# A fused retention and SoLU kernel: four more activation tiles transposed by DMA, the extra load buffers one stage sooner, and the orders of all engines renewed from the fifth step on

## The chip, the cores and the metric

The kernel runs on one core of a Trainium2 chip. A core has five engines that run side by side and meet at semaphores: TensorE (PE, matrix products; PEld is its row of weight loads), VectorE (DVE), ScalarE (ACT), GpSimd (POOL) and SyncE (SP, which here issues nearly all transfers to the 16 DMA engines). The metric is device time in microseconds (us), less is better.

## The reference

Two parts follow each other. The first is attention with a decay (retention) for 8 batches and 8 heads, a sequence of 576 and a head size of 64. The second takes the 4608 tokens by 512 features that come out, multiplies by `w_in` (512 x 1024), applies SoLU (h times its softmax), normalizes, scales with `g_ln` and multiplies by `w_out` (1024 x 512).

```python
scores = scale * np.matmul(q, k.transpose(0, 1, 3, 2))
Dmat = np.where(rel >= 0, gamma[:, None, None] ** rel[None, :, :], 0.0)
ret = np.matmul(scores * Dmat[None, :, :, :], v)
...
h = x @ w_in
e = np.exp(h - h_max)
sm = e / (np.sum(e, axis=-1, keepdims=True) + 1e-09)
solu = h * sm
ln = (solu - mu) / np.sqrt(var + 1e-06) * g_ln
out = ln @ w_out
```

All inputs and the output are float32; the matrix products run in float16 with sums in float32.

## The kernel before

**Stages and tiles.** The retention is cut into 18 windows. Sixteen hold 256 positions of one batch, two (the last of each half of the batches) gather the 64 positions that remain of four batches. Each window is done in two halves of four heads: 36 stages. Each window then gives two tiles of 128 tokens for the second part: 36 tiles. The two run interleaved, a stage runs some three steps ahead of the tile with the same number.

A stage i consists of these operations (in brackets the lines in the code that the profile shows):
- `ldq`, `ldk`, `ldv` (L462, L467): loads of q, k and v by SP, into five `raw` buffers of each kind, or, for the stages that `extra(i)` names, into three more (`bis`). These three take the space of the buffers through which the weights came in, so they cannot be used before `w2_center` (`wc`, L853) has read the last of these.
- `sq`, `sk`, `cv` (L477, L482): scaling of q and k with the decay and the cast of v to float16, most of it on POOL, a few of the first ones on DVE and ACT.
- `T` (L509 in the first ten stages, L519 later): PE transposes q and k; `Te` or `TL` (L547, L549) on ACT copies the result from PE's memory to an `ev` buffer, of which there are eight.
- `S` (L619): the scores, into the bank `s`; `mask` (L655) on DVE multiplies with the mask.
- `K` (L579): the update of the state from k and v; `st`, `sm`, `sc` (L679 to L682, L687, L696) carry it on, on DVE and POOL.
- `I` and `V` (L579): the part from the state and the part from the scores, summed in the bank `xy`; `xe` (L701) on ACT casts the result to `xT`.

A tile t consists of these:
- `M1` (L712): eight matmuls with `w_in` into the bank `h`; `ex` (L720), the exponential, on ACT; `so` (L735, L730), the product, on DVE, which frees `h`. There is a single `h`, so M1 of a tile waits for `so` of the tile before.
- the statistics: `bnA`, `bnB` (L741, L743) on DVE or `va` (L749) on ACT, then `fx`, `fin` and `rs` (L758, L764, L775).
- the transpose of solu, in one of two ways. Either PE does it (`L`, L531 for the first four and the last tile, L538 with 32 narrow matmuls for the others) and ACT copies it out; or, for the tiles in the list `LX`, one DMA transpose does it (`lx`, L567), issued by SP, from the buffer of solu straight to an `ev` buffer. Where PE does it in the steady part, tile t shares one transposed block and one copy (`TL`, 128x1024) with stage t + 6; where it doesn't, stage t + 6 is copied alone (`Te`, 128x512).
- `M2` (L785): eight matmuls with `w_out`, most of the time into the same bank `s` that the scores use, so that `S` waits for the copy before it; `oe` (L794) on ACT scales and copies the result, `out` (L805, L810) stores it.

**What sets the order.** The order of every engine is written out by hand in `ORDER` (L53 to L110), a string of names for each engine. `plan()` gives each operation its dependencies and its buffers; `order_ops` merges the five lists into one order of emission with a table of durations. Engines run their lists strictly in order, and SP's list is also the order in which transfers are issued. So an operation that waits holds up everything behind it in its own list. `LX` (L42) and `R0` (L44) are read by `ev_T`, `ev_L` and `extra`:

```python
def ev_T(i):
    return f"tx{i}" if i in TX else f"Te{i}" if i < NJ + 2 or i - 6 in LX else f"TL{i - 2}"
...
def extra(i):
    return i >= R0 and (i - R0) % 8 >= 5
```

With `R0 = 10`, stages 15 to 17, 23 to 25 and 31 to 33 are loaded into the extra buffers. With `LX` from 14, tiles 14 to 34 are transposed by DMA; tiles 4 to 13 are transposed on PE together with stages 10 to 19. In the list of PE, a step from M1 to M1 looks like this in the part where PE transposes solu, and like this later:

```
M1_11 M2_7 I14 L10 V14 T16 S15 M1_12
...
M1_24 M2_20 I27 T29 V27 K29 S28 M1_25
```

Of the kernel before, what the change touches and what calls it, by code (L numbers as in the profile page):

```python
# [12 lines left out]
I32 = mybir.dt.int32  # L13
# [4 lines left out]
for _b in range(0, B, 4):  # L18
# [20 lines left out]
)  # L39


LX = (14, 15, 16, 17, 18, 19, 20, 21, 22, 23, 24, 25, 26, 27, 28, 29, 30, 31, 32, 33, 34)  # L42
TX = ()
R0 = 10  # L44
OT = 30
SPL = ()
TWO = ()
# [4 lines left out]

ORDER = dict(  # L53
    PE=(
# [11 lines left out]
    ),  # L66
    ACT=(
# [9 lines left out]
    ),  # L77
    DVE=(
# [9 lines left out]
    ),  # L88
    POOL=(
# [8 lines left out]
    ),  # L98
    SP=(
# [9 lines left out]
    ),  # L109
)  # L110

# [8 lines left out]
def ev_T(i):  # L120
    return f"tx{i}" if i in TX else f"Te{i}" if i < NJ + 2 or i - 6 in LX else f"TL{i - 2}"


def ev_L(t):
    return f"lx{t}" if t in LX else f"Le{t}" if t < NJ - 4 or t + 6 >= NS or t + 6 in TX else f"TL{t + 4}"


def extra(i):
    return i >= R0 and (i - R0) % 8 >= 5

# [18 lines left out]
def plan():  # L149
# [3 lines left out]
    def op(name, eng, kind, deps, key, bufs=(), moved=0.0):  # L153
        eng = ON.get(name, eng)
        dur = DUR[kind[eng] if isinstance(kind, dict) else kind] if not isinstance(kind, float) else kind
        ops.append(Op(name, eng, dur, deps, rank.get(name, OFF + PER * key[0] + key[1]), bufs, moved))

    for i in range(NS):
# [21 lines left out]
        else:  # L180
            sdep = [f"sc{2 * (w - 8 + 2 * r + 1) + hf}" for r in range(4)]
        jn, alone = i >= NJ + 2, i - 6 in LX
        if i in TX:
# [15 lines left out]
    for t in range(NT):  # L199
# [4 lines left out]
        op(f"ex{t}", "ACT", "ex", [f"M1_{t}"], (m, 3.3), [("e", [f"so{t}"])])  # L204
        op(f"so{t}", "DVE", "soA" if va else "so", [f"ex{t}"], (m, 4.56), [("solu", [f"lx{t}" if t in LX else f"L{t}", f"va{t}" if va else f"bnB{t}"])])
        if va:
# [10 lines left out]
        early = t < NJ - 4  # L217
        if t in LX:
            op(f"lx{t}", "SP", "lx", [f"so{t}"], (m + 2, 0.1), [("ev", [f"M2_{t}"])], DUR["ltx"])
        lasts = [x for x in range(NT) if NJ - 4 <= x < OT and ev_L(x)[:2] == "Le"]  # L220
        after = [f"Te{NJ + 1}", f"Le{NJ - 5}"] if t == NJ - 4 else []
        if t in lasts:
            after += [f"Le{t - 2}" if t - 2 in lasts else ev_T(max(i for i in range(NS) if i not in TX))]
        if t not in LX:
            op(f"L{t}", "PE", "Lw" if wide(f"L{t}") else "L", [f"so{t}"] + after, (m + 2, 0.1),
# [855 lines left out]
```

## Time and profile before

| | |
|---|---|
| median of 3 runs | 210.38 us (209.81 to 211.48) |
| the profiled execution | 210.31 us |
| its span, first to last instruction | 208.6 us |
| PE, DVE, ACT, POOL busy | 95%, 73%, 68%, 67% of the span |
| PE's clock granted | 0.999 of full speed |
| HBM read, written | 32.56 MB, 9.44 MB |

The profile is of one execution. An engine's busy time counts its own instructions, not the waits, the branches or the issue of transfers. In the timeline a row is one instruction or several of a kind in a row: start, length, engine, line, operation, what is written from what, with shapes and the count; in brackets stands the idle time before it and what ended that. A row of windows gives for one stretch of time the busy time of each engine and the number of its instructions. The share of DMA is the time of the packets that start in the stretch over 16 engines, and so can pass 1 where packets queue.

### The profile page before, as it was taken

The numbers are of one execution on the slowest core, as the hardware profiler recorded it, in microseconds if no ns is written. First come the engines' busy times: TensorE is split into PE (matmuls) and PEld (weight loads), VectorE is DVE, ScalarE is ACT, GpSimd is POOL, SyncE is SP. The second block draws the span as 40 slices with busy tenths as digits, with TensorE's granted clock in tenths as the row PEclk, the third lists the DMA queues.
The fourth block names the chain that finished last, engine by engine and source line by source line (L and its number), as shares of the span: only waits on it lengthen the run. The fifth ranks groups of instructions, "written<-read, shape, count | busy, mean of one in ns | idle before, by whom it ended". The sixth has DMA issues, their size and how long they took to land. (4 is left out here: it accounts for less than half of the span.)

```text
span 208.6 us, 8795 instructions
## 1 busy us (share of the span) xinstructions
PE 197.4 (95%) x3704; PEld 109.3 (52%) x3704; DVE 151.7 (73%) x269; ACT 142.6 (68%) x250; POOL 139.9 (67%) x235
## 2 busy tenths in 40 slices
PE   7998898899999999999999999999999999999981
PEld 2353553665555556566555555555565555544441
DVE  6476868996868788688876877687688787728550
ACT  2367677898667667766787678667768966468441
POOL 7444648999995999677559997996996593201110
PEclk9999999999999999999999999999999999999999
DMA  6999999999756766999999999989997869917834
GB/s 164 340 361 300 326 314 264 301 294 304 226 169 199 205 191 207 287 293 284 201 304 286 221 290 237 225 217 288 220 155 213 198 162 187 175 53 172 142 141 104
DMA packets 86889, 48.09 MB, mean 231 GB/s; under 512 B 25400, under 2 KB 80704, under 8 KB 86848
## 3 DMA queue, kind: packets, MB, share of 16 engines
q1 hardware_dynamic: 86608, 47.33, 90.9%
q8 instruction: 29, 0.48, 1.0%
q10 hardware_dynamic: 240, 0.18, 0.4%
q14 instruction: 12, 0.10, 0.2%
HBM read 32.56 MB, written 9.44 MB: 201 GB/s over the span
## 5 line engine op out<-in xcount | busy, mean ns | idle before, releaser
L712 PE MATMUL h_ps<-w_in,xT 128*128 128x512 f16 x288 | 68.6, 380 | 0.2 <-ACT xT L701 0.2
L785 PE MATMUL o_ps<-w2c,ev 128*128 128x512 f16 (+1 forms) x296 | 67.6, 373 | 0.0
L655 DVE TENSOR_TENSOR ret<-s_ps,masks 128x1024 f16<-128x1024 f32 x36 | 43.8, 1218 | 13.1 <-PE s_ps L619 13.0
L720 ACT ACTIVATE e_sb<-h_ps 128x1024 f32<-128x1024 f32 x36 | 36.8, 1023 | 17.6 <-PE h_ps L712 17.0
L785 PEld LDWEIGHTS <-ev 128*128 128x128 f16 x296 | 28.8, 98 | 32.9
L477 POOL TENSOR_TENSOR k<-rawk,small 128x512 f16<-128x512 f32 x34 | 35.3, 1046 | 8.9 <-DMA rawk<-in_k_dram 8.4
L712 PEld LDWEIGHTS <-xT 128*128 128x128 f16 x288 | 25.4, 98 | 29.6 <-ACT xT L701 1.0
L735 DVE TENSOR_TENSOR solu<-h_ps,e_sb 128x1024 f16<-128x1024 f32 x22 | 26.9, 1222 | 17.7 <-ACT e_sb L720 17.7
L794 ACT ACTIVATE o_sb<-o_ps,rs 128x512 f32<-128x512 f32 (+1 forms) x37 | 24.8, 675 | 21.8 <-PE o_ps L785 10.2
L477 POOL TENSOR_TENSOR q<-rawq,small 128x512 f16<-128x512 f32 x34 | 35.3, 1043 | 5.6 <-DMA rawq<-in_q_dram 5.0
L701 ACT CAST xT<-xy 128x512 f16<-128x512 f32 x36 | 26.4, 735 | 4.9 <-PE xy L579 4.7
L741 DVE BATCH_NORM_STATS2 bs<-solu 128x6 f32<-128x512 f16 x44 | 29.5, 682 | 0.1
L696 POOL CAST sbd<-gg 64x256 f16<-64x256 f32 x64 | 25.3, 395 | 2.6
L549 ACT COPY ev<-tl 128x512 f32<-128x512 f32 (+1 forms) x26 | 19.5, 749 | 2.7 <-PE tl L519 2.5
L730 DVE SCALAR_TENSOR_TENSOR solu<-h_ps,e_sb 128x1024 f16<-128x1024 f32 x14 | 17.1, 1223 | 5.0 <-ACT e_sb L720 3.8
L775 POOL TENSOR_TENSOR rs<-w,small 128x2 f32<-128x2 f32 x18 | 12.4, 690 | 11.6 <-DVE w L764 10.6
L482 POOL CAST v<-rawv 128x512 f16<-128x512 f32 x28 | 17.0, 610 | 3.8 <-DMA rawv<-in_v_dram 3.5
L687 POOL TENSOR_TENSOR gg<-gt,small 128x128 f32<-128x128 f32 x32 | 13.1, 409 | 6.6 <-DVE gt L682 6.5
L773 POOL TENSOR_TENSOR w<-mv,w 128x2 f32<-128x2 f32 x11 | 2.1, 195 | 22.8 <-DVE mv L743 8.0
L749 ACT ACTIVATE junk<-solu,su 128x1024 bf16<-128x1024 f16 x14 | 16.1, 1149 | 0.1
L619 PE MATMUL s_ps<-ev 64*64 64x128 f16 x576 | 15.1, 220 | 0.5 <-ACT o_sb L794 0.2
L579 PE MATMUL xy<-ret,v 64*64 64x128 f16 x576 | 15.0, 220 | 0.1
(73 smaller groups left out, 216.1 us busy)
## 6 DMA issues: line engine op xcount, KB each, us to landing
rawq<-in_q_dram SPq DMA_DIRECT2D x32, 256.0 KB, 5.3
rawk<-in_k_dram SPq DMA_DIRECT2D x32, 256.0 KB, 5.5
rawv<-in_v_dram SPq DMA_DIRECT2D x32, 256.0 KB, 5.4
out_dram<-o_sb SPq DMA_DIRECT2D x32, 256.0 KB, 3.7
wst<-in_moe_w_in_dram SPq DMA_DIRECT2D x4, 512.0 KB, 6.7
wst<-in_moe_w_out_dram SPq DMA_DIRECT2D x4, 512.0 KB, 8.6
rawq<-in_q_dram SPq DMA_DIRECT2D x16, 64.0 KB, 3.4
rawk<-in_k_dram SPq DMA_DIRECT2D x16, 64.0 KB, 3.2
```

Of the source, the lines that this page charges most:

```text
L477: eng.tensor_tensor(out=t.rearrange("p j h d -> p h j d"), in0=st[i]["r" + nm], in1=g, op=ALU.mult)
L549: nc.scalar.copy(out=t[:, lo:hi].rearrange("p x (r w) -> p r x w", r=2), in_=tls[n].rearrange("p r x w -> p (r x w)").bitcast(FP).rearrang ...
L655: nc.vector.tensor_tensor(out=d["ret"].rearrange("p e h j q -> p (e h) (j q)")[:, :, 0:n], in0=d["s"].rearrange("p e h j q -> p (e h) (j q ...
L696: nc.gpsimd.tensor_copy(out=t[ee[e], :, :, ee[e]], in_=st[i]["gg"][ee[e]])
L701: nc.scalar.copy(out=xT[:, 2 * w : 2 * w + 2, 2 * hf : 2 * hf + 2].rearrange("p c h (q j) -> p c h j q", j=2), in_=xys[i][:, :, 0:256].rea ...
L712: nc.tensor.matmul(out=h_ps[:, hh], lhsT=xT[:, t, dc], rhs=w_in16[:, dc, hh], start=(dc == 0), stop=(dc == 3),)
L720: nc.scalar.activation(out=d["e"], in_=d["h"], func=ACT.Exp, accum_out=se[:, t : t + 1])
L730: nc.vector.scalar_tensor_tensor(out=d["solu"], in0=d["h"], scalar=1.0, in1=d["e"], op0=ALU.mult, op1=ALU.mult, accum_out=d["su"],)
L735: nc.vector.tensor_tensor(out=d["solu"], in0=d["h"], in1=d["e"], op=ALU.mult)
L741: nc.vector.bn_stats(out=d["bs"][:, half], in_=d["solu"][:, half * 512 : half * 512 + 512])
L785: nc.tensor.matmul(out=o, lhsT=d["ev"][:, d["lo"] + c], rhs=w2c16[:, c, mm], start=(c == 0), stop=(c == 7))
L794: nc.scalar.activation(out=d["osb"][:, mm], in_=d["o", half], func=ACT.Copy, scale=ws[t // 2]["rs"][:, t % 2 : t % 2 + 1])
```

## The change

1. `LX` begins with 10 instead of 14: tiles 10 to 13 are transposed by DMA too. Their `L` leaves PE (128 narrow matmuls), `TL14` to `TL17` on ACT become `Te16` to `Te19`, and `lx10` to `lx13` come into the list of SP.
2. `R0` is 9 instead of 10: the extra load buffers serve stages 14 to 16, 22 to 24 and 30 to 32.
3. `ORDER` is written anew. The lists agree up to `M1_3` on PE, `Te5` on ACT, `so1` on DVE, `sq4` on POOL and `ldq6` on SP, and differ in many places after that.

The core of the diff, with the part of the lists where they begin to differ and where the four transposes stand (in the lists of the diff, lines that go on are cut):

```diff
-LX = (14, 15, 16, 17, 18, 19, 20, 21, 22, 23, 24, 25, 26, 27, 28, 29, 30, 31, 32, 33, 34)
+LX = (10, 11, 12, 13, 14, 15, 16, 17, 18, 19, 20, 21, 22, 23, 24, 25, 26, 27, 28, 29, 30, 31, 32, 33, 34)
 TX = ()
-R0 = 10
+R0 = 9
...
PE
-M1_3 T5 K7 T6 I4 S5 V4 T7 I5 S6 V5 T8 M1_4 I6 S7 V6 K8 T9 L2 M2_0 I7 L3 V7 K9 S8 M1_5 M2_1 I8 L4 V8 K10 S9 T10
+M1_3 K7 T5 I4 V4 S5 T6 I5 V5 S6 T7 M1_4 T8 I6 S7 V6 K8 L2 T9 M2_0 L3 I7 V7 S8 K9 M1_5 M2_1 I8 V8 L4 T10 K10 S9
...
-M1_11 M2_7 I14 L10 V14 T16 S15 M1_12 M2_8 I15 L11 V15 T17 S16 M1_13 M2_9 I16 V16 L12 T18 K18 S17
+M1_11 M2_7 I14 T16 V14 S15 M1_12 M2_8 I15 V15 T17 S16 M1_13 M2_9 I16 V16 K18 T18 S17
-M1_14 M2_10 I17 L13 V17 T19 S18 K19 M1_15
+M1_14 M2_10 I17 T19 V17 K19 S18 M1_15
ACT
-Te5 va2 Te6 xe4 fx1 fx0 Te7 xe5 va0 Te8 ex4 xe6 Le2 va3 oe0 xe7 Le3 Te9 ex5 oe1 TL8 xe8 ex6
+Te5 va0 xe4 Te6 fx1 xe5 fx0 Te7 va3 va2 Te8 xe6 Le2 ex4 oe0 Te9 xe7 ex5 Le3 oe1 xe8 TL8 fx2 ex6
POOL
-sk4 sq4 sk6 sm4 sc4 sk5 sm6 sk7 sm5 sq5 sc5 sq6 sq7 sk8 sq8 sk9 sc6 cv8 sq9 sm7 sc7 rs0 sq10
+sk4 sq4 sm4 sk6 sk5 sc4 sm6 sk7 sq5 sm5 sc6 sq6 sc5 sq7 sq8 cv8 sk8 sq9 sk9 sm7 cv9 rs0 sc7
...
-sc9 sq12 sm10 sq13 sk14 sk13 sc10 sk12 cv12 sm11 rs2 cv13 sc11 sq15
+sc9 sq12 sm10 sk12 cv12 sc10 sk14 sm11 rs2 sk13 sq14 cv15 sc11 sq13
SP
-out4 ldv17 out6 out5 ldv19 ldq19 ldk19 ldk20 ldv20 ldq20 ldv21 ldq22 ldk21 out8 out7 ldq21 ldv22 ldk22
+out4 ldq17 ldv20 ldv19 ldq19 ldq20 ldk19 ldk20 out5 out6 lx10 ldq21 ldv21 ldk21 ldk23 ldv23 ldq23 lx11 out7
+ldv22 ldk22 lx12 out8 out9 ldq22 ldq24 ldk25 out10 ldk24 lx13 ldv24 ldq25 ldk26 lx14
```

Nothing else is changed: the operations, their shapes, the numbers of buffers and the code that emits them are the same.

88 rows, old and new, of tables (ACT, DVE, PE, POOL) are left out of this document.

## The prediction

> **What bounds the kernel now.** I read the page's first two parts, then the stages by windows, then one step of the timeline.
>
> ```profile
> span 208.6 us, 8795 instructions
> ...
> PE 197.4 (95%) x3704; PEld 109.3 (52%) x3704; DVE 151.7 (73%) x269; ACT 142.6 (68%) x250; POOL 139.9 (67%) x235
> ...
> DMA  6999999999756766999999999989997869917834
> ```
>
> PE is busy for 95% of the span, and its gaps lie in the start and the tail. The DMA digits show full load up to slice 10, slack in slices 10 to 15 (52 to 83 us), and full load again after that. A step of the pipeline runs from one M1 (the eight w_in matmuls, L712) to the next, and step t begins with M1_t. The windows below are steps 11 to 14, the last four in which PE transposes a solu tile (L10 to L13); after them come the sums of steps 15 to 18 and of 28 to 30, where the queue of SP does it by DMA. Columns: length, busy time and count of each engine, PE clock, DMA share, GB/s.
>
> ```profile
> 79.30:84.19 4.89, 4.89 (x127) 2.80 (x116) 3.60 (x6) 3.77 (x8) 4.77 (x8) 1.00 0.80 249
> 84.19:89.42 5.23, 5.09 (x123) 2.87 (x117) 3.86 (x5) 3.42 (x6) 3.46 (x6) 1.00 1.03 280
> 89.42:94.49 5.07, 5.07 (x142) 3.04 (x137) 4.58 (x7) 3.11 (x6) 3.24 (x5) 1.00 0.99 291
> 94.49:99.51 5.02, 5.02 (x142) 3.04 (x137) 3.64 (x8) 3.62 (x7) 4.27 (x8) 1.00 0.98 292
> sum 20.21, PE 20.07 PEld 11.75 DVE 15.68 ACT 13.92 POOL 15.74; mean PE 5.02 PEld 2.94 DVE 3.92 ACT 3.48 POOL 3.93
> ...
> sum 19.23, PE 19.23 PEld 10.81 DVE 15.30 ACT 14.92 POOL 13.94; mean PE 4.81 PEld 2.70 DVE 3.83 ACT 3.73 POOL 3.48
> ...
> sum 14.36, PE 14.36 PEld 7.91 DVE 10.85 ACT 10.22 POOL 8.97; mean PE 4.79 PEld 2.64 DVE 3.62 ACT 3.41 POOL 2.99
> ```
>
> PE fills both kinds of step, and no other engine reaches its length except POOL and DVE in single steps. With the transposes on PE four steps take 20.21 us; without them, 19.23, and later 14.36 / 3 = 4.79 each. What sets 4.79 is seen inside a step: first one with L (step 11), then one without (step 29).
>
> ```profile
> 81.04 1.89 PE L785 MATMUL o_ps<-w2c,ev 128*128 128x512 f16 x8
> ...
> 82.97 0.69 ACT L794 ACTIVATE o_sb<-o_ps,rs 128x512 f32<-128x512 f32 x1 [0.61 <-PE o_ps L785]
> ...
> 83.08 0.45 PE L538 MATMUL tl<-ident,solu 64*64 64x64 f16 x32
> ...
> 83.36 0.40 PE L579 MATMUL xy<-ret,v 64*64 64x128 f16 x16
> ...
> 83.83 0.43 PE L619 MATMUL s_ps<-ev 64*64 64x128 f16 x16
> ...
> 84.19 1.90 PE L712 MATMUL h_ps<-w_in,xT 128*128 128x512 f16 x8
> ```
>
> ```profile
> 166.58 1.90 PE L712 MATMUL h_ps<-w_in,xT 128*128 128x512 f16 x8
> ...
> 168.32 1.89 PE L785 MATMUL o_ps<-w2c,ev 128*128 128x512 f16 x8
> ...
> 170.25 0.69 ACT L794 ACTIVATE o_sb<-o_ps,rs 128x512 f32<-128x512 f32 x1 [0.55 <-PE o_ps L785]
> ...
> 170.99 0.42 PE L619 MATMUL s_ps<-ev 64*64 64x128 f16 x16
> ...
> 171.34 0.61 PE L712 MATMUL h_ps<-w_in,xT 128*128 128x512 f16 x2
> ```
>
> L takes 83.36 - 83.08 = 0.28 us of PE. But the scores S (L619) share one buffer with M2's output, so S cannot start before the copy o_sb (L794) has freed it. In step 29 S starts 0.05 us after o_sb ends (170.94), in step 11 it starts 0.17 after (83.66). So a step without L has a floor: 1.74 from M1 to M2, 2.67 from M2 to S, 0.35 from S to the next M1, together 4.76. Part of L's 0.28 us is hidden under that copy already.
>
> [...]
>
> **The change, part by part.**
>
> *LX from 10: PE.* It takes 4 x 32 narrow transposes off PE, in steps 11 to 14. By the pitch that is 4 x 0.28 = 1.12 us; by the floor the four steps become 4 x 4.79 = 19.16, a gain of 20.21 - 19.16 = 1.05. Of this, 0.27 us is a stall of PE's instruction issue in step 12, which has nothing to do with L:
>
> ```profile
> 88.61 0.21 PEld L579 LDWEIGHTS <-v 64*64 64x64 f16 x12 [0.27 <-issue]
> ```
>
> Whether it moves with the instructions is unknown; between 0 and 0.27 I take that it comes back elsewhere. Term: **-0.8** (ends -0.5, if only the S slack of 0.17 and the like is won, and -1.05).
>
> *LX from 10: ACT and buffers.* Four joint copies of q, k and solu become copies of q and k alone, half the size. ACT is busy 13.92 of these 20.21 us, so this is worth nothing on the path. Each of the four tiles now holds two ev buffers instead of half of one; steps 15 to 18 already run that way with PE full. Term: 0.
>
> *LX from 10: DMA and SP.* Four transposes join the one queue of SP.
>
> ```profile
> 77.46 1.22 DVE L735 TENSOR_TENSOR solu<-h_ps,e_sb 128x1024 f16<-128x1024 f32 x1 [0.64 <-ACT e_sb L720]
> ...
> 78.80 1.58 SPq L805 DMA_DIRECT2D out_dram<-o_sb  x2
> ...
> 96.22 1.89 PE L785 MATMUL o_ps<-w2c,ev 128*128 128x512 f16 x8
> ```
>
> ```profile
> L567 SPq DMA_TRANSPOSE ev<-solu x21: 1232/1287/3354, 99.5 to 194.8; - x21
> ...
> DMA to landing us min/median/max: 3.9/4.6/5.9
> ```
>
> solu of tile 10 is done at 78.68, and lx10 stands in the list right behind out6, issued at 78.80. So it goes out near 79.3 to 80.4 and lands 3.9 to 5.9 us later, by 86.3; M2_10 wants it at 96.22. That leaves 10 us to spare, and lx11 to lx13, placed 5 us or more ahead of their M2, have less but enough. Issuing them holds SP for 4 x 1.3 us (up to 4 x 3.4), with the loads of stages 21 to 25 queued behind. Their price on the DMA engines, from windows without and with transposes:
>
> ```profile
> 55.00:80.00 25.00, 24.88 (x656) 14.58 (x655) 19.98 (x34) 17.86 (x29) 22.04 (x38) 1.00 0.62 180
> 80.00:100.00 20.00, 19.86 (x505) 11.66 (x504) 15.49 (x24) 13.71 (x24) 15.47 (x24) 1.00 0.97 282
> 100.00:155.00 55.00, 55.00 (x1100) 30.57 (x1099) 42.70 (x76) 41.53 (x75) 45.49 (x76) 1.00 1.18 244
> ```
>
> Loads and stores cost 0.97 x 20 / (0.282 x 20) = 3.44 us per MB. The last window holds 13.4 MB in 64.9 us of share, with 11 transposes (2.9 MB): 64.9 - 10.5 x 3.44 = 28.8, an estimate of 2.6 us each, so four cost 10.4 us. The idle share before 80 us is 25 x 0.38 = 9.5 us. The new SP list uses it: the loads of stages 17, 19 and 20 now stand ahead of out5 and out6, which kept SP until 78.80. So I take the transposes as covered. Term: 0 (ends -0.2 and +4, below).
>
> *R0 = 9.* Stages 14, 15, 16 (then 22 to 24, 30 to 32) use the extra load buffers instead of 15 to 17 and so on; the first three buffers open one stage sooner. They wait for the w2 centering on DVE, which ends a few tenths later. It lets loads run earlier where DMA is idle and is worth nothing by itself. Term: 0.
>
> *New orders, steps 3 to 5.* On PE, T8 moves from before M1_4 to behind it; K7, I4 and V4 move up. On POOL sk8 and sk9 move back by 2.5 us of work, on ACT ex4 goes behind xe6 and Le2.
>
> ```profile
> 42.15 1.91 PE L712 MATMUL h_ps<-w_in,xT 128*128 128x512 f16 x8
> ...
> 44.09 1.02 ACT L720 ACTIVATE e_sb<-h_ps 128x1024 f32<-128x1024 f32 x1
> ...
> 46.26 0.58 ACT L547 COPY ev<-tl 128x512 f32<-128x512 f32 x1 [0.43 <-PE tl L531]
> ...
> 46.62 1.21 DVE L735 TENSOR_TENSOR solu<-h_ps,e_sb 128x1024 f16<-128x1024 f32 x1
> ...
> 49.25 0.61 PE L712 MATMUL h_ps<-w_in,xT 128*128 128x512 f16 x2
> ```
>
> M1_4 can start some 0.3 us sooner (its last input comes after V5, which moves up), but T8 then costs 0.46 between M1_4 and M1_5. ex4 starts when Le2 ends, at 46.84; with 1.1 us it ends at 47.95, so4 takes 1.21 to 49.2, and M1_5, whose bank so4 frees, starts at 49.25 as before. In before so4 ended at 47.83, 1.42 us ahead; that margin is used up. Term: 0 (ends -0.3 and +1.1).
>
> *New orders, steps 5 to 10 and the rest.* L stays on PE in steps 5 to 10 with the same work; only who stands last before M1 differs, 0.1 us a step in both directions. On POOL, sq13 falls back by 9 us of work and then ends about 1 us ahead of T13, the thinnest place that I find; further on, sq23 and sk23 come forward. Steps 15 to 35 and the tail hold the same work. Term: 0 (ends -0.3 and +0.5).
>
> **Sum.** The profiled execution took 210.31 us, 1.71 beyond its span; the median of the runs shown is 210.38, so nothing is lost in going from one to the other. 210.31 - 0.8 = **209.5 us**.
>
> **The rivals.**
>
> *A. The margin of ex4 breaks (slower).* Place: Le2, ex4, so4, M1_5 near 47 to 49 us. Every delay of T8, xe6 or L2 now goes one to one into M1_5 and from there to the end. ex4 moves behind 2.5 us of ACT work with 1.42 us of margin: at most +1.1, so 210.31 - 0.8 + 1.1 = 210.6. It outweighs the gain once M1_5 starts after 50.05. For it: POOL's sk8 and sk9, which T8 and T9 need, come late by 2.5. Against it: both still end just before PE reaches them.
>
> *B. The transposes starve the loads (slower).* If the idle share cannot be used because loads wait for buffers, everything behind lx10 lands up to 10.4 us later, into steps where POOL has no time to catch up:
>
> ```profile
> 99.51:104.27 4.76, 4.76 (x108) 2.68 (x99) 4.14 (x8) 3.64 (x6) 2.20 (x5) 1.00 0.96 194
> 104.27:109.07 4.80, 4.80 (x105) 2.64 (x99) 3.82 (x7) 4.16 (x10) 2.40 (x4) 1.00 1.13 307
> ...
> 113.94:118.74 4.80, 4.80 (x101) 2.71 (x101) 4.07 (x7) 3.50 (x8) 4.80 (x7) 1.00 1.19 202
> ```
>
> POOL's idle 2.56 + 2.40 us is swallowed first, and T23 follows its q with 0.8 us to spare: 10.4 - 5.0 - 0.8 = 4.6 us, so 210.31 - 0.8 + 4.6 = 214.1. It decides from a lateness of 5.8 us; half way between, 211.8. Against it: the loads pulled ahead of out5 and out6. [...]
>
> *C. Nothing is won.* If o_sb's copy, not PE, times the steps with L too, they stay and the time is 210.3. Against it: S comes 0.17 us after o_sb in step 11 and steps 15 to 18 are shorter by a quarter microsecond each.
>
> *D. More is won.* The stall of 0.27 vanishes and the reordered steps 5 to 10 lose their own: 209.5 - 0.3 - 0.4 = 208.8.
>
> **How the numbers follow.** Forecast (209.0 to 210.1) 0.52; A 0.15; B 0.14, of which half beyond 212.5; C 0.11; D 0.08. The predicted time is the forecast's 209.5. The range runs from 208.6 (most of D) to 212.0 (A, C and the milder B) and leaves out under 0.2. A measurement of this kernel tells about 1% from no change, so faster means under 208.3 (a part of D, 0.05), slower over 212.5 (half of B and an unforeseen wait, 0.13), and the rest, 0.82, is within 1%.
>
> **What would show it.** Right: four steps of about 4.8 us where L10 to L13 stood, S starting 0.05 us after o_sb in each, lx10 to lx13 landing before M2 wants them, M1_5 near 49.25. Wrong: a wait of h_ps for so4 near 49 us (A); POOL waiting for rawq or rawk after 85 us and tl waiting for POOL (B); PE gaps before T13; a transposed ev awaited by M2.

## The result, and the profile after

The changed kernel takes 211.56 us (median of 20 executions, 210.26 to 213.7) against 209.99 us (20 executions) for the kernel before on the same chip. The ratio is 1.0074, 95% interval 1.0053 to 1.0096. That is slower by 0.74%, about 1.6 us, where the prediction had 0.8 us of gain. It stayed within the predicted range, but on the other side of no change. Here and below, the ratios leave out executions that took over 1.5% more than the fastest of their kernel.

The execution of the changed kernel that was profiled first took 213.7 us, the slowest of its 20, and held a stall that is told of at the end. So the comparison uses the profile of a second series of the same kernel, called `after_again`, of 212.54 us (the median of that series is 211.57). Its page, with the lines that answer to those shown of the kernel before:

```profile
span 210.8 us, 8542 instructions
...
PE 197.3 (94%) x3576; PEld 109.2 (52%) x3576; DVE 151.2 (72%) x269; ACT 140.6 (67%) x250; POOL 139.4 (66%) x235
...
PEclk9999999799999999999999999999999999999999
DMA  6999999999868569999999999999999995954734
```

PE issues 128 matmuls less, as it should, and yet is busy for as long as before (197.3 against 197.4 us). The digit 7 in the row of its clock says why: at the eighth digit, near 40 us, the clock was granted only in part. The windows of the two kernels show where the time went. Each stretch begins where an M1 begins; the rows are steps 3, 4, 5 to 10, 11 to 14, 15 to 19, 20, and 21 to the end. First `after_again`:

```profile
33.83:43.78 9.95, 7.90 (x129) 4.80 (x121) 7.57 (x14) 5.74 (x13) 9.67 (x15) 0.83 1.10 294
43.78:51.21 7.43, 7.43 (x155) 5.18 (x153) 5.39 (x10) 6.79 (x14) 4.72 (x9) 1.00 1.11 291
51.21:80.95 29.74, 29.74 (x794) 17.28 (x785) 25.61 (x42) 20.52 (x33) 26.05 (x44) 1.00 0.75 210
80.95:100.30 19.35, 19.33 (x383) 10.81 (x377) 15.56 (x23) 12.95 (x25) 16.27 (x26) 1.00 1.17 254
100.30:124.18 23.88, 23.88 (x501) 13.38 (x495) 18.45 (x33) 17.19 (x32) 19.67 (x33) 1.00 1.19 248
124.18:130.22 6.04, 4.88 (x106) 2.73 (x100) 3.77 (x7) 5.48 (x12) 5.76 (x11) 1.00 1.31 185
130.22:210.80 80.58, 75.05 (x1154) 40.31 (x1153) 52.54 (x93) 51.17 (x94) 38.79 (x67) 1.00 0.85 193
```

And the same stretches of the kernel before, except for steps 11 to 14, whose 20.21 us stand in the prediction:

```profile
34.50:42.15 7.65, 6.95 (x138) 4.35 (x130) 7.17 (x13) 5.93 (x14) 7.04 (x10) 1.00 1.13 299
42.15:49.25 7.10, 6.92 (x148) 4.53 (x145) 5.65 (x10) 6.17 (x12) 6.79 (x12) 1.00 1.14 293
49.25:79.30 30.05, 29.93 (x791) 17.56 (x785) 24.48 (x40) 21.07 (x34) 27.01 (x46) 1.00 0.70 205
...
99.51:123.50 23.99, 23.99 (x504) 13.49 (x495) 19.01 (x34) 18.05 (x33) 18.55 (x31) 1.00 1.11 261
123.50:128.30 4.80, 4.80 (x105) 2.66 (x99) 3.71 (x6) 4.11 (x8) 4.38 (x9) 1.00 1.25 204
128.30:208.60 80.30, 75.01 (x1161) 40.17 (x1154) 53.14 (x93) 52.62 (x97) 40.75 (x70) 1.00 0.87 181
```

The difference, in order: M1_3 starts 0.67 us sooner (33.83 against 34.50), step 3 takes 2.30 us more, step 4 takes 0.33 more, steps 5 to 10 take 0.31 less, steps 11 to 14 take 0.86 less, steps 15 to 19 0.11 less, step 20 takes 1.24 more, and the rest 0.28 more. The sum is 2.20, the difference of the spans (210.8 - 208.6). So the gain that was predicted is there, and two losses that were not are larger: one at 40 us and one at 128 us.

Three of these sizes vary from execution to execution. M1_3 also starts at 33.41 in another profile with the old orders (`before_solu5`, below), so its 0.67 us can't be put down to the change. And in the first profile of the changed kernel steps 3 and 4 together take 16.66 us (1.91 more than before, against 2.63 more in `after_again`), and step 20 takes 4.99 (only 0.19 more).

**Step 3.** The timeline of PE in the kernel before, from the end of M1_3 on (the two rows of q belong to T5 and T6, L619 is S5; L970 are dummy matmuls that keep PE at work):

```profile
36.77 0.40 PE L509 MATMUL tl<-ident,q 128*128 128x128 f16 x4 [0.38 <-POOL q L477]
...
37.57 1.04 PE L970 MATMUL wm<-zeros 128*128 128x512 f16 x4
38.69 0.40 PE L509 MATMUL tl<-ident,q 128*128 128x128 f16 x4
...
39.35 0.42 PE L619 MATMUL s_ps<-ev 64*64 64x128 f16 x16
```

And of `after_again`, first PE, then one row of DVE:

```profile
37.30 0.29 PE L579 MATMUL xy<-ev,sbd 128*128 128x128 f16 x2 [0.58 <-DVE gt L682]
...
37.77 0.39 PE L619 MATMUL s_ps<-ev 64*64 64x128 f16 x16
39.58 1.82 PE L970 MATMUL wm<-zeros 128*128 128x512 f16 x4 [1.42 <-DVE ret L655]
41.18 0.63 PE L509 MATMUL tl<-ident,q 128*128 128x128 f16 x4
```

```profile
38.30 1.22 DVE L655 TENSOR_TENSOR ret<-s_ps,masks 128x1024 f16<-128x1024 f32 x1
```

A line that the diff does not touch explains it. The table `FILL` (L50) has the entry `'T6': (2, 4)`: four dummy matmuls are emitted ahead of T6, into bank number 2, which is the bank `s` of the scores. Before, T6 stood ahead of S5, the bank was free, and the dummies filled a moment in which PE had nothing else. In the new order S5 stands ahead of T6. Now the dummies want the bank that S5 has just written, and wait until mask5 (L655) has read it: 1.42 us, in which PE could have gone on with T6. Ahead of that stands a second wait of 0.58 us: K7, moved up, takes the one bank `xy`, and I4 must wait until the state update has read it. Then, in this execution, PE runs at half clock, as the length of the same matmuls shows (four dummies 1.82 instead of 1.04 us, T6 0.63 instead of 0.40), and as the window on the stretch says:

```profile
39.66:43.07 3.41, 3.41 (x38) 2.03 (x41) 1.83 (x3) 0.69 (x2) 3.41 (x5) 0.50 1.20 299
```

**Step 20.** SP's queue in `after_again` (the rows are lx18, out14 and lx17), then DVE, then PE:

```profile
121.26 2.03 SPq L567 DMA_TRANSPOSE ev<-solu  x1
123.38 0.54 SPq L805 DMA_DIRECT2D out_dram<-o_sb  x1
124.01 1.30 SPq L567 DMA_TRANSPOSE ev<-solu  x1
```

```profile
128.94 1.22 DVE L735 TENSOR_TENSOR solu<-h_ps,e_sb 128x1024 f16<-128x1024 f32 x1 [2.09 <-DMA ev<-solu]
```

```profile
130.22 1.02 PE L712 MATMUL h_ps<-w_in,xT 128*128 128x512 f16 x4 [1.16 <-DVE solu L735]
```

The new list of SP has lx17 behind lx18 and out14; before, it stood ahead of both. There are four buffers of solu, and a tile that is transposed by DMA keeps its buffer until the transpose has read it. so20 is given the buffer of tile 17 (the semaphore that it waits on is lx17's). So DVE sits idle for 2.09 us, and M1_21, which needs the bank `h` that so20 frees, waits 1.16 us.

The predicted terms for the path itself hold. L10 to L13 are gone, and S follows the copy of o_sb, here in step 11 (o_sb ends at 85.30, S starts 0.14 us later, behind the V that the new order has there):

```profile
84.61 0.69 ACT L794 ACTIVATE o_sb<-o_ps,rs 128x512 f32<-128x512 f32 x1 [0.61 <-PE o_ps L785]
...
85.44 0.39 PE L619 MATMUL s_ps<-ev 64*64 64x128 f16 x16
```

### The profile page after: what moved, and what is told of

Its sections match the earlier page's. It is cut to its first block, busy times and chain, and to the rows that moved or that the text cites. A ratio compares the mean times of both kernels' runs of the same rounds, so it can differ in the third digit from the quotient of the medians.

```text
span 212.0 us, 8542 instructions
## 1 busy us (share of the span) xinstructions
PE 197.6 (93%) x3576; PEld 109.2 (51%) x3576; DVE 151.7 (72%) x269; ACT 140.6 (66%) x250; POOL 139.7 (66%) x235
## 5 line engine op out<-in xcount | busy, mean ns | idle before, releaser
L712 PE MATMUL h_ps<-w_in,xT 128*128 128x512 f16 x288 | 69.8, 386 | 0.2
L655 DVE TENSOR_TENSOR ret<-s_ps,masks 128x1024 f16<-128x1024 f32 x36 | 43.9, 1221 | 14.3 <-PE s_ps L619 14.2
L712 PEld LDWEIGHTS <-xT 128*128 128x128 f16 x288 | 26.0, 99 | 30.5 <-issue 2.1
L549 ACT COPY ev<-tl 128x512 f32<-128x512 f32 (+1 forms) x26 | 17.7, 680 | 3.5 <-PE tl L519 3.4
L619 PE MATMUL s_ps<-ev 64*64 64x128 f16 x576 | 15.3, 222 | 0.6 <-ACT ev L547 0.2
```

What stands on the lines that cost most here:

```text
L549: nc.scalar.copy(out=t[:, lo:hi].rearrange("p x (r w) -> p r x w", r=2), in_=tls[n].rearrange("p r x w -> p (r x w)").bitcast(FP).rearrang ...
L655: nc.vector.tensor_tensor(out=d["ret"].rearrange("p e h j q -> p (e h) (j q)")[:, :, 0:n], in0=d["s"].rearrange("p e h j q -> p (e h) (j q ...
L712: nc.tensor.matmul(out=h_ps[:, hh], lhsT=xT[:, t, dc], rhs=w_in16[:, dc, hh], start=(dc == 0), stop=(dc == 3),)
```

## The experiments

Three theories were tried against each other: that the new orders of steps 3 and 4 cost the time, that the place of lx17 and the number of solu buffers do, and that the four transposes or the loads around them do. A fourth, that stalls of PE's instruction issue do, was aimed at by one run (loads later). `R0` = 9 was never run by itself, so its term of 0 stays untested. The theories are numbered in the expectations, each of which says what its theory is. The kernel before took 210.16, 210.04 and 210.25 us in the three sets (medians of 23, 27 and 29 executions).

**The changed kernel again.** No edit.

> The changed kernel unaltered, as the control of the other three. In its first profile PE lost time at three places: 2.67 us from S5 to T6 (0.3 to 0.4 is usual), 1.85 us before L7 with no semaphore named, and 1.43 us in M1_9, which ran at half clock. Theory I (a late fetch of PE's instructions behind loads that were pulled forward): the gap before L7 comes and goes from run to run, and so does a stretch of half clock behind it; 210.3 us where it is missing, 211.5 as the median. Theory F (the four fill matmuls tied to T6 wait for the mask of stage 5): the wait before T6 is there in every run. Rival X (the DMA transposes themselves cost): steps 11 to 14 would be longer than 4.8 us each.

211.57 us, ratio 1.0063 (1.0035 to 1.009). The loss is confirmed. Its profile is the one above.

**Without the dummy matmuls ahead of T6.**

```diff
-FILL = {..., 'K6': (0, 1), 'T6': (2, 4)}
+FILL = {..., 'K6': (0, 1)}
```

> The changed kernel without the entry T6 in the table of fills, so without four of the dummy matmuls that keep PE busy (they compute nothing of the result). Theory F: T6 starts right after S5 and its q, 2.2 us sooner; the input of M1_4 then sets it, 1.5 us sooner, and about 0.6 to 0.9 us are left at M1_5, because w2's centering and sq10 on POOL then hold PE: 210.6 to 210.9 us against 211.5 for the changed kernel. If the fill is harmless: 211.5. If the idle PE drops its clock instead: 212 or more.

210.96 us, ratio 1.0021 (0.9986 to 1.0055). PE in step 3:

```profile
38.19 0.40 PE L579 MATMUL xy<-ev,sbd 128*128 128x128 f16 x2 [0.67 <-DVE gt L682]
...
38.95 0.64 PE L619 MATMUL s_ps<-ev 64*64 64x128 f16 x16
39.52 0.61 PE L509 MATMUL tl<-ident,q 128*128 128x128 f16 x4
```

The wait of 1.4 us is gone and M1_5 starts at 49.66, but step 3 still takes 8.80 us: the waits of K7 (for the cast of v) and I4 remain (1.37 and 0.67 us here) and so does a stretch of half clock (S takes 0.64 us here, 0.39 in `after_again`). The dummies are one part of the loss in step 3, not all of it. By the times alone even this part is not settled: the interval of this ratio meets that of the changed kernel (1.0035 to 1.0090).

**The transposes alone.** The kernel before with `LX` from 10, L10 to L13 taken out of PE's list and lx10 to lx13 put into SP's; every other order, and `R0`, as before.

```diff
 PE
-I14 L10 V14 T16 ... I15 L11 V15 T17 ... V16 L12 T18 ... I17 L13 V17
+I14 V14 T16 ... I15 V15 T17 ... V16 T18 ... I17 V17
 ACT
-TL14 ... TL15 ... TL16 ... TL17
+Te16 ... Te17 ... Te18 ... Te19
 SP
-ldv20 ldq20 ... out8 out7 ... ldk22 ldq24 ... out9 ldq23
+ldv20 lx10 ldq20 ... out8 lx11 out7 ... ldk22 lx12 ldq24 ... out9 lx13 ldq23
```

> The kernel before with the four DMA transposes alone: LX from 10, L10 to L13 out of PE's list, TL14 to TL17 replaced by Te16 to Te19, and lx10 to lx13 put into SP's list a few transfers ahead of where they are needed; R0 and all other orders as before. If the prediction's term is right (a step without L costs 4.79 us), it is 0.8 us faster than before: 209.2 against 210.0. Rival X (the transposes starve the loads): 210.5 or more, with POOL waiting for q or k after 85 us.

216.04 us, ratio 1.0281 (1.0245 to 1.0316). Steps 11 to 14 take 4.76, 4.80, 4.81 and 5.01 us, so the gain on PE is there. It is lost many times over in steps 18 and 19 (9.62 and 6.85 us). ACT, then PE:

```profile
121.83 0.69 ACT L794 ACTIVATE o_sb<-o_ps,rs 128x512 f32<-128x512 f32 x1 [5.26 <-DMA out_dram<-o_sb]
```

```profile
122.57 0.64 PE L619 MATMUL s_ps<-ev 64*64 64x128 f16 x16 [4.47 <-ACT o_sb L794]
123.15 3.60 PE L712 MATMUL h_ps<-w_in,xT 128*128 128x512 f16 x8
```

o_sb waits for one of its three buffers, since the stores that free them stand behind loads in SP's list. S waits for o_sb, and half clock follows (M1 takes 3.60 instead of 1.90 us).

**The transposes alone, with the stores ahead of the loads.**

```diff
 SP
-ldq25 ldk25 ldq27 ldk27 ldq26 ldv26 ldk26 ldv27 out11 out12 lx15 out13
+ldq25 out11 ldk25 ldq27 ldk27 ldq26 out12 lx15 ldv26 ldk26 ldv27 out13
```

> The kernel before with the four transposes and R0 = 10, as in lx_alone, but with the stores out11 and out12 (and lx15) moved ahead of six loads in the list of SP. If the place of the stores alone cost lx_alone its 6 us (o_sb waits for an output buffer that a store frees, S for o_sb, and the clock falls to half after that wait): step 18 falls from 9.62 to about 5, no half clock between 120 and 128 us, and the time is 209 to 210. If the four transposes themselves overload the DMA engines, loads come late instead: POOL waits for q or k in steps 17 to 22, and the time stays above 212.

215.85 us, ratio 1.0288 (1.0239 to 1.0336). Step 18 falls to 4.80 us, but steps 19 and 20 take 6.19 and 9.00, and the time is the same. PE now waits for the transposes themselves, twice:

```profile
121.10 1.90 PE L786 MATMUL o_ps<-w2c,ev 128*128 128x512 f16 x8 [1.26 <-DMA ev<-solu]
...
128.67 3.28 PE L786 MATMUL o_ps<-w2c,ev 128*128 128x512 f16 x8 [2.64 <-DMA ev<-solu]
```

So the place of the two stores decided which step paid, and not how much was lost. In these two runs with the old list of SP (216.04 and 215.85 us) the four more transposes were too much for the queue, and whatever stood last paid. Where the time goes it is M2 that waits, for the transposes, and not POOL for its loads, as had been expected. That the new list of SP, with loads pulled into the idle time before 80 us, is what lets the changed kernel carry the transposes is likely, but argued only: its DMA share between M1_5 and M1_11 is 0.75 against 0.70, and no run has the four transposes with the new list of SP and all else as before.

**Loads later.** The changed kernel, with the loads of stages 17 and 18 some places further back in SP's list.

```diff
 SP
-out1 ldv18 ldq18 ldk17 out2 ldv17 ldk18 out3 out4 ldq17
+out1 out2 ldk17 out3 ldv18 out4 ldv17 ldq18 ldk18 ldq17
```

> The changed kernel with the loads of k17, v18, q18, v17 and k18 moved 2 to 8 us back in SP's list, behind out2, out3 and out4, so that DMA is not full from 64 to 68 us. Theory I: the gap before L7 and the stretch of half clock behind it go, 210.3 us in most runs instead of 211.5. If the gap has another cause (the order of PE, L7's tile), it stays and the time is 211.5.

213.23 us, ratio 1.0132 (1.0095 to 1.0169). The stall near 71 us that it was aimed at does not show, but it does not show in the unaltered kernel's second profile either, so this tells nothing of its cause. All that stands behind the loads goes out later; in the profiled execution, one of 216.44 us, step 20, with the same wait of so20 for lx17, takes 8.16 us. This expectation on the time was missed.

**lx17 ahead.** The changed kernel with one move.

```diff
 SP
-lx16 ldq26 ldv28 lx18 out14 lx17 ldk29 lx19
+lx16 lx17 ldq26 ldv28 lx18 out14 ldk29 lx19
```

> The kernel after with one move in the list of SP: lx17 directly behind lx16, ahead of four loads, lx18 and out14. Theory II (so20 waits for the solu buffer that lx17 frees, and M1_21 with it): so20 follows ex20 within 0.1 us instead of 2.1, step 20 falls from 6.03 us to 4.8 to 5.0, and the time by 1.1 us, from 211.57 to about 210.4. Rival (the wait is taken over by the next late thing, such as the loads of stages 26 and 28 now behind lx17, or the output buffers): step 20 gets short, but steps 21 to 25 give it back, and the time stays at 211.2 to 211.8.

210.63 us, ratio 1.0021 (0.9992 to 1.005). In the profile, which is of the slowest of the ten executions (213.28 us), so20 waits for its exponential only, and step 20 takes 4.80 us; but so17 now waits for a buffer (that of lx14), and M1_18 0.47 us for so17:

```profile
115.33 1.22 DVE L735 TENSOR_TENSOR solu<-h_ps,e_sb 128x1024 f16<-128x1024 f32 x1 [1.67 <-DMA ev<-solu]
```

Most of the expected 1.1 us came (0.9 by the medians), though the interval of the ratio meets that of the changed kernel (1.0035 to 1.0090).

**Steps 3 and 4 as before.** The changed kernel, with all five lists as before up to M1_5, oe1, mask8, rs0 and ldv9.

```diff
 PE
-M1_3 K7 T5 I4 V4 S5 T6 I5 V5 S6 T7 M1_4 T8 I6 S7 V6 K8 L2 T9 M2_0 L3 I7 V7 S8 K9 M1_5
+M1_3 T5 K7 T6 I4 S5 V4 T7 I5 S6 V5 T8 M1_4 I6 S7 V6 K8 T9 L2 M2_0 I7 L3 V7 K9 S8 M1_5
```

> The kernel after, with the orders of steps 3 and 4 on all engines as they were before (PE up to M1_5, ACT up to the copy oe1, DVE up to mask8, POOL up to rs0, SP up to ldv9); the transposes of tiles 10 to 13 by DMA, R0 and all orders after that stay. Theory I (the new order of steps 3 and 4 costs 2 us, by the dummy matmuls ahead of T6 that wait for mask5, K7 and I4 waiting for the one xy bank, and the half clock that follows): M1_5 starts near 49.3 instead of 51.2, no stretch of half clock between 38 and 44 us, and the time falls by 1.5 to 2.0 us to 209.6 to 210.1. Rival (the later steps cost it: the loads in flight hold M1_5 back to its place, or stalls of instruction issue move elsewhere): M1_5 near 49.3, but the time above 210.8.

M1_5 starts at 48.60 instead of 51.21, with no half clock (1.00 in the windows of steps 3 and 4). The times fall apart: five executions took 209.25 to 212.24 us, and six took 212.77 to 215.51, so the median of all is 212.77. The ratio, from the five alone, is 1.0001 (0.9959 to 1.0043). The profile is of one of the six (212.77 us), and where its 2.6 us went is seen there: M1_18 waits 1.36 us, M1_21 0.67 and M1_33 0.65, 2.7 us together, each for a so that waits for a solu buffer. Here is so17:

```profile
112.88 1.22 DVE L736 TENSOR_TENSOR solu<-h_ps,e_sb 128x1024 f16<-128x1024 f32 x1 [2.48 <-DMA ev<-solu]
```

The expectation on the cause held. That on the time held for the five executions (the ratio puts them at 210.1 us) and failed for the median of all. In the profiled execution PE gets to tile 17 sooner, but the queue of transposes does not, so the time won at 45 us is given back from 110 us on. None of the five was profiled; that they are faster because so waits less there is likely, but not shown.

**Both edits.** Steps 3 and 4 as before, and lx17 ahead.

> Both edits at once: the orders of steps 3 and 4 as before, and lx17 directly behind lx16. If the two costs are separate and add up (1.5 to 2.0 and 1.1 us): 208.5 to 209.0, 1.2 to 1.7 us under the kernel before, the shorter steps 11 to 14 (0.9) and 5 to 10 (0.3) being what is left. If they overlap, or the stalls of instruction issue set the rest: 209.8 to 210.6, the same as the kernel before.

209.54 us, ratio 0.9983 (0.9945 to 1.0021). No wait of M1_21 is left, and 0.48 us of M1_18. That is the same as the kernel before, short of the 208.5 to 209.0 of the better expectation. But the interval lies below that of the changed kernel (1.0035 to 1.0090): these two repairs together take its loss away.

**A fifth buffer of solu.** The changed kernel with:

```diff
-    e=2, solu=4, osb=3,
+    e=2, solu=5, osb=3,
```

> The kernel after with five buffers of solu instead of four; nothing else. Theory II (from step 15 on, so waits for a solu buffer that a queued transpose still reads): so17, so18 and so20 start within 0.1 us of their exponential, M1_18 and M1_21 no longer wait, steps 17 to 20 take 4.75 to 4.9 us each, and the time falls by 1.2 to 1.7 us from that of after, to about 210.0 to 210.4. Rival (the transposes land late whatever the buffers): the wait moves on to M2 (a transposed ev awaited by PE) or to the ev buffers, and the time stays within 0.5 us of after.

In the profile it does what was expected: steps 15 to 20 take 4.75 to 4.81 us each, and no M1 waits.

```profile
100.69:124.56 23.87, 23.87 (x501) 13.34 (x494) 18.45 (x33) 17.18 (x32) 19.69 (x33) 1.00 1.15 223
124.56:129.37 4.81, 4.81 (x106) 2.70 (x99) 3.71 (x6) 4.25 (x9) 4.59 (x9) 1.00 1.12 199
```

The time does not follow: 211.46 us, ratio 1.0048 (1.0016 to 1.008), where 210.0 to 210.4 was expected. In this execution step 3 took 10.93 us, 0.98 more than in `after_again`, because K7 waited 1.04 us for the cast of v. With the new order step 3 took 8.80 to 10.93 us in the profiles of seven runs; with the old one 7.65 to 7.87 in seven. Before that cast ACT waited 1.77 us here, and 0.70 in `after_again`, for the load of v. So the new order makes step 3 depend on when a load lands as well; whether that alone hides the microsecond won later in the median is not settled by one profile.

**The new orders of steps 3 and 4 alone.** The kernel before, with the five lists of the changed kernel up to the same places (on POOL up to sc7); `LX`, `R0` and all later orders as before.

```diff
 PE
-M1_3 T5 K7 T6 I4 S5 V4 T7 I5 S6 V5 T8 M1_4 I6 S7 V6 K8 T9 L2 M2_0 I7 L3 V7 K9 S8 M1_5
+M1_3 K7 T5 I4 V4 S5 T6 I5 V5 S6 T7 M1_4 T8 I6 S7 V6 K8 L2 T9 M2_0 L3 I7 V7 S8 K9 M1_5
```

> The kernel before with the new orders of steps 3 and 4 alone (PE up to M1_5, ACT up to oe1, DVE up to mask8, POOL up to sc7, SP up to ldv9 as in the kernel after; LX from 14, R0 = 10 and all later orders as before). Theory I: M1_5 starts at 50.5 to 51.5 instead of 49.3, the dummy matmuls ahead of T6 wait for mask5, half clock follows for 3.4 us, and the time is 1.5 to 2.0 us above the kernel before, 211.6 to 212.1. Rival (the loss of steps 3 and 4 is absorbed later, by loads that are ready the earlier): M1_5 late, but the time within 0.5 us of before.

212.7 us, ratio 1.0109 (1.0062 to 1.0157): 2.3 us slower, a little more than expected. The same signs stand in its profile (and a wait of 0.48 us of K7 for the cast of v):

```profile
37.01 0.28 PE L579 MATMUL xy<-ev,sbd 128*128 128x128 f16 x2 [0.66 <-DVE gt L682]
...
39.28 1.87 PE L970 MATMUL wm<-zeros 128*128 128x512 f16 x4 [1.41 <-DVE ret L655]
```

M1_5 starts at 50.91. This settles the first theory: these lists by themselves make the kernel slower by about as much as the whole change does (the two intervals overlap). Which of the five lists it takes was not tried apart.

**The control: the kernel before with five buffers of solu.**

> The kernel before with five buffers of solu: the control. If it is the change that turned the solu buffers into a limit, the time is the same as that of the kernel before (210.0, within 0.3 us). If the fifth buffer helps whatever the orders, it falls by 0.5 us or more.

209.56 us, ratio 0.9984 (0.9951 to 1.0017): not to be told from no change, but a gain of 0.5 us is not ruled out either. The profiles say more: with four buffers as with five, no M1 waits for a so in them. With transposes from tile 14 on, the buffers were not what bound the kernel in those two executions.

**All three repairs.** Steps 3 and 4 as before, lx17 ahead, five buffers of solu; what is left of the change is `LX` from 10, `R0` = 9 and the later orders.

> The orders of steps 3 and 4 as before, lx17 directly behind lx16, and five buffers of solu. In the version with the first two edits, 0.48 us of wait for solu was left ahead of M1_18 and about 0.2 us in steps 16 and 22. If the fifth buffer takes these away: 208.6 to 209.1, under the kernel before by 0.5 to 0.7%. If the DMA queue itself is the limit from 100 to 125 us: M2 waits for a transposed ev instead, and the time stays at 209.4 to 209.9.

209.3 us, ratio 0.9956 (0.9926 to 0.9987): faster than the kernel before by 0.9 us, and the only version of all that is. (From the control it cannot be told.) Its windows, in the order of those above:

```profile
33.17:41.04 7.87, 7.01 (x139) 4.36 (x129) 7.39 (x14) 6.24 (x14) 7.46 (x10) 1.00 1.16 290
41.04:48.15 7.11, 6.90 (x148) 4.61 (x145) 5.53 (x9) 5.96 (x12) 6.80 (x13) 1.00 1.13 290
48.15:79.22 31.07, 29.92 (x792) 17.35 (x785) 25.63 (x42) 20.80 (x34) 25.79 (x44) 1.00 0.81 226
79.22:98.35 19.13, 19.13 (x382) 10.76 (x377) 15.54 (x23) 12.84 (x25) 16.27 (x26) 1.00 1.21 256
98.35:122.23 23.88, 23.88 (x501) 13.36 (x494) 18.44 (x33) 17.20 (x32) 19.67 (x33) 1.00 1.22 249
122.23:127.03 4.80, 4.80 (x105) 2.64 (x98) 3.71 (x6) 4.24 (x9) 4.58 (x9) 1.00 1.24 233
```

Steps 11 to 14 take 19.13 us, where the prediction had 19.16 (4 x 4.79). Steps 4 and 15 to 20 are what they were before, and step 3 is 0.2 us longer. The third row holds one wait of 1.15 us of S for o_sb in step 8, which the profile of the version without the fifth buffer doesn't have; without it this execution would be that much shorter still.

## Why the prediction was wrong

*"LX from 10: PE", term -0.8: right.* Steps 11 to 14 went from 20.21 to 19.35 us (-0.86), in other versions to 19.13. In two, `no_fill` and `lx17_first`, a stall of instruction issue (1.21 and 0.96 us) fell into step 11, and the four steps took 20.39 and 20.15; so the prediction did well to keep back a part for such stalls. Rival C, by which nothing is won where L goes, did not come true. The floor of 4.76 us, read from M1, M2, o_sb and S, held in every step from 11 to 30 that nothing else disturbed.

*"LX from 10: DMA and SP", term 0: right for the landing, but incomplete.* The new list of SP does carry the transposes, and no load behind them came late enough to stop PE. The two runs with the old list show what the price can be: they end 6 us above the kernel before, where rival B had 3.8 (4.6 less the gain of 0.8), and by other waits than B's. But the step looked at the ev buffers that a transpose fills and at the loads behind it, and not at the solu buffer that it keeps. That belongs to *"ACT and buffers"*, where only ev was counted.

*"New orders, steps 3 to 5", term 0: this is the step that failed.* It measured +1.96 us at M1_5 (51.21 against 49.25), beyond the upper end of +1.1. Without the chance in the start of M1_3, steps 3 and 4 took 2.63 us more, and 1.91 in the first profile. Rival A named the right place and the wrong mechanism: M1_5 waited for nothing, and ex4 was no limit. The working followed the operations that moved and asked when their inputs were ready, but not which bank each of them writes, nor what is emitted along with it. S5 ahead of T6 moves the four dummies behind a reader of their bank; K7 ahead of T5 takes the one `xy` before I4 and wants v7 before it is cast. Half clock followed there in every profile of these orders but the first: it lasted 3.41 us in `after_again` and `late_loads`, and the four dummies took 1.82 us in `after_again`, 1.86 in `solu5` and 1.87 in `early_alone`, instead of 1.04. `early_alone` shows these orders at +2.3 us by themselves.

*"New orders, steps 5 to 10 and the rest", term 0 (ends -0.3 and +0.5): right for 5 to 10, wrong for the rest.* Steps 5 to 10 gave -0.31, the lower end. Step 20 cost +1.24 in this profile (+0.19 in the first), through the place of lx17. Of the 0.28 us of the rest, 0.27 lie behind M1_35, as they do in every version with `LX` from 10; their cause stays open. The prediction said that steps 15 to 35 hold the same work, and did not follow SP's list there, where lx17 had been moved behind lx18 and out14.

*The sum.* -0.86 for the steps that lost their L, -0.31 and -0.11 for those beside them, +1.96 up to M1_5, +1.24 for step 20, +0.28 for the rest: +2.2 us in this profile, 1.3 to 1.6 us by the two ratios. That 211.56 fell inside the range was luck: its upper end stood for rival A and the milder rival B, and neither is what happened. Rival D's reordered steps 5 to 10 came true as well, but on the wrong side of larger losses.

## What to carry to other kernels

When an order moves, follow each moved instruction to the bank or buffer that it takes and the last reader of it, and count what is emitted along with it, dummy work above all: filler placed for one order becomes a wait in another (1.42 us ahead of T6 here). A transfer that reads a buffer in place of an engine holds that buffer until it has gone through its queue (so20 waited 2.09 us for lx17); ask how many buffers stand between producer and queue before asking how long the transfer takes. And time won upstream of a queue that is full can be given back at that queue: the profiled execution of `early_before` won 2.6 us at 48 us and lost 2.7 after 110.

## What the runs showed of the hardware

**Behind short waits PE ran at half clock for 3.41 us, in some profiles.** Waits of 0.58 and 1.42 us in a row stood ahead of it in `after_again`, and the stretch at 0.50 lasted 3.41 us. In the first profile of the changed kernel one of 1.85 us stood ahead of a stretch of the same length: here are PE, and the window.

```profile
70.89 0.45 PE L538 MATMUL tl<-ident,solu 64*64 64x64 f16 x32 [1.85 <-issue]
...
71.96 3.34 PE L712 MATMUL h_ps<-w_in,xT 128*128 128x512 f16 x8
```

```profile
71.48:74.89 3.41, 3.41 (x38) 1.35 (x25) 2.48 (x5) 1.65 (x2) 0.06 (x1) 0.50 0.81 260
```

A wait of 1.16 us ahead of M1_21 in `after_again` was not followed by any (the first four matmuls of M1_21 took 1.02 us, and the window from there on has 1.00). Nor were waits of 0.66 and 1.42 us in step 3 of the first profile, almost the same as those of `after_again`: the dummies behind them took 1.02 us, not 1.82. So the length of the waits alone does not decide it.

```profile
39.46 1.02 PE L970 MATMUL wm<-zeros 128*128 128x512 f16 x4 [1.42 <-DVE ret L655]
```

What does decide it no run here tests. Where half clock followed, behind a wait of 1.85 us or of 0.58 and 1.42, it cost 1.7 us of PE's work (half of 3.41).

**Five stalls of PE fall on records whose numbers differ by multiples of 256.** The wait of 1.85 us above has no releaser but "issue": its inputs had long been ready. Such stalls stand in several of the profiles, at different operations (1.21 us in `no_fill`, 0.46 in `before_solu5`). Counted from the first record of PE and its weight loads, the sequencer's own records included, five of them fall on numbers 2242 (the one above), 3010, 3266, 3778 and 4034, each 194 more than a multiple of 256, in kernels with different lists. Another of them, in `early_alone` (number 3778):

```profile
101.69 0.38 PE L579 MATMUL xy<-ret,v 64*64 64x128 f16 x13 [1.13 <-issue]
```

The pages list a DMA queue of kind instruction, q8, with 29 packets (0.48 MB) in the kernel before and 28 (0.46 MB) in `after_again`. PE has 3704 matmuls and as many weight loads in the one, 3576 and as many in the other: in both 255 to a packet, close to the 256 of the spacing. That a packet came late at these stalls was not shown: Theory I in the expectation of `after_again`, a late fetch behind loads, was only argued, and the run aimed at it told nothing. The stall of 0.27 us that the prediction met in step 12 is one of these (number 3266; 0.27 is the idle time of the weight loads; PE itself was idle for 0.14 us of that step).
